# Gated recurrence and mixture layer on one core: GpSimd's parts of the weights given to ScalarE and VectorE, with a new order, engine shares and PSUM banks

## The chip, the cores and the metric

One NeuronCore of a Trainium2 chip runs the whole kernel. The metric is the device time in microseconds (us) of one execution, median over several runs; less is better.

## The reference

The first half is a decayed outer-product recurrence over 768 steps for 4 batches and 8 heads of width 48; its rows, 3072 tokens of 384 values, go through a gated layer of width 1536.

```python
for t in range(S):
    state = alpha[:, :, t, :, None] * state + einsum('bhd,bhe->bhde', k[:, :, t], v[:, :, t])
    y[:, :, t] = einsum('bhd,bhde->bhe', q[:, :, t], state)
x = y.transpose(0, 2, 1, 3).reshape(3072, 384)
g = x @ w_gate
out = (g * sigmoid(g) * (x @ w_val)) @ w_out
```

q, k, v and alpha are 32-bit floats. The three weights come as 64-bit floats, so the kernel reads each as two 32-bit words and makes a float of them itself.

## The kernel before, in words

**Recurrence.** The 768 steps of 4 batches are cut into 16 units of T = 192 steps (3 chunks of 64). A unit u loads alpha, k, q (La, Lk, Lq) and v (V), turns them so that the head dimension lies on partitions (on TensorE for units 0 to 3: T, K, with the widening copies p; on VectorE later: tr, tk, tq, kr), forms decay products by two scans on VectorE (G: `backward`, f: `forward`), multiplies k and q by them (mk, q), and lets TensorE form the scores (S), the carried state (Bw, or inside S) and the outputs (Y). VectorE masks (ma), advances and decays the state (ad, de); values are copied by vc. The output rows are scaled into an upper and a lower half-precision part (yh on ScalarE, yl on VectorE) and repacked into the x tile of a block (R and x on TensorE for units 0 and 1, copies xr by SyncE later).

**Layer.** Tokens form 7 blocks of 384 or 512. For each block, 12 steps f run over the width in slices of 128: `product` makes g and v with nine matmuls each (three row groups, each as upper x upper, upper x lower, lower x upper parts of half precision), `silu` (sl, ScalarE) and `hidden` (h, VectorE) make the gated value, `hidden_hi` and `hidden_lo` (hh, hl) split it, `out_product` (o) adds nine matmuls to the outputs. Step s = 12 x block + f; the names are g0, v0, ..., o83. There are two buffers each for h, hh and hl.

**Weights.** 36 slices of weights form 20 groups w0 to w19 (w0, w1, w2 and w19 of one slice, 384 columns; the others of two, 768). A group n is loaded (`wl`), made a float in three steps (v0, v1, v2; `single`), then split: `high` writes the upper part a, scaled by 256 to half precision; `low` writes the lower part p, the scaled value less the upper one. On VectorE `low` is one instruction (L353); on GpSimd it is two, a scaling in place (L355) and a subtraction (L356). Three spare tiles hold floats between v0 and p. All 20 groups are made while the first block (steps 0 to 11) is computed. Raw words of group n lie in the place of group n + 1, Y0 and Y1 lie in that of w18 and w17, and the tile for the widening copies in that of w19.

**Order.** The whole program stands in the text `ORDER` (L85): words such as `g:w13p` name the engine (t TensorE, v VectorE, s ScalarE, g GpSimd, y SyncE, whose queue issues nearly all loads) and the piece of work; digits behind @ are the PSUM banks, of A0, A1, A2, ops0, ops1, vps, gps, ops2 (0 to 7). Each engine works through its words in this order, and waits by semaphores for the data it needs. vps and gps are also the banks of the products v and g.

**Checks.** Beside the work ScalarE tests that weights and alpha lie in a range (wc, ck) and squares the hidden values (sq) of one step per block and of all of the last block. The results are joined (fr, fa, fe) into a flag by `verdict` (fb), which all engines read (fl, L1181) to branch past a slow general path (L1349).

Of the kernel before, what the change touches and what calls it, by code (L numbers as in the profile page):

```python
# [8 lines left out]
F32 = mybir.dt.float32  # L9
# [137 lines left out]
def main_path(ctx, tc, q, k, v, alpha, w_gate, w_val, w_out, out, flag, spill):  # L147
# [172 lines left out]

    idle, taken, read = ["t", "A", "B"], {}, []
    negative = {x for n, pieces in enumerate(wgroups) if f"g:w{n}v1" in ORDER.split() for x in pieces}

    def weight_group(n, pieces):

        size = len(pieces) * NB  # L330
        is32 = w_gate.dtype == F32
        each = NB if is32 else 2 * NB

        shape, dt = [P, len(pieces) * each], F32 if is32 else U32
        if n + 1 < len(wgroups):
            raw = p2.tile(shape, dt, tag=f"w{n + 1}", bufs=1, name=f"raw{n}")
        else:
            raw = spare(idle[0], shape, dt, f"raw{n}")
            taken["raw", n] = idle.pop(0)
        for i, piece in enumerate(pieces):  # L340
            weight_dma(raw[:, i * each : (i + 1) * each], *piece)
        parts = []

        def high(eng, src):
            parts.append(pairs16(p2.tile([P, 2 * size], F32, tag=f"w{n}", name=f"w{n}", bufs=1), [P, 2, size]))
            for i, piece in enumerate(pieces):
                wsp[piece] = tuple(parts[0][:, x, i * NB : (i + 1) * NB] for x in range(2))
            scaled(nc, eng, parts[0][:, 0, :], src, W_SCALE)

        def low(eng, src):  # L350
            hi, lo = parts[0][:, 0, :], parts[0][:, 1, :]
            if eng is nc.vector:
                eng.scalar_tensor_tensor(out=lo, in0=src, scalar=W_SCALE, in1=hi, op0=ALU.mult, op1=ALU.subtract)  # L353
            else:
                eng.tensor_scalar(out=src, in0=src, scalar1=W_SCALE, scalar2=None, op0=ALU.mult)  # L355
                eng.tensor_tensor(out=lo, in0=src, in1=hi, op=ALU.subtract)  # L356
            if n in taken:
                idle.append(taken.pop(n))

        if is32:  # L360
            return [], [lambda eng: high(eng, raw)], [lambda eng: low(eng, raw)]
        raw = raw.rearrange("p (c two) -> p c two", two=2)
        t = []

        def cut(i, eng):
            if not i:
# [509 lines left out]
    def hidden(blk, f):  # L876
        h = acc["h", blk, f]
        v_ = acc.pop(("v", blk, f))
        if (("v", f) in negative) != (("o", f) in negative):
            nc.vector.scalar_tensor_tensor(out=h, in0=v_, scalar=-1.0, in1=h, op0=ALU.mult, op1=ALU.mult)  # L880
        else:
            nc.vector.tensor_tensor(out=h, in0=h, in1=v_, op=ALU.mult)  # L882

    def hidden_hi(blk, f, eng):
        tag, n = ("tr", 1) if (blk, f) == (NBLK - 1, NF - 1) else ("hh", NH)
        hh = acc["hh", blk, f] = p2.tile([P, BLOCKS[blk][1]], F16, tag=tag, name=f"hh{blk}_{f}", bufs=n)
        (eng.copy if eng is nc.scalar else eng.tensor_copy)(out=hh, in_=acc["h", blk, f])  # L887

    def hidden_lo(blk, f, eng):
# [3 lines left out]
        eng.tensor_tensor(out=hl, in0=acc.pop(("h", blk, f)), in1=hh, op=ALU.subtract)  # L893
        hT[blk, f] = (hh, hl)

    squares = {}

    def squared(blk, f):

        h = acc["hh", blk, f]  # L900
        if f == 0:
            squares[blk] = p2.tile([P, BLOCKS[blk][1]], BF16, tag=f"sq{blk}", name=f"sq{blk}", bufs=1)
# [478 lines left out]
```

## Time and profile before

| | before |
|---|---|
| runs, us | 547.59, 548.43, 549.39 (median 548.43) |
| profiled execution, us | 548.03, its span 546.2 |
| busy us: VectorE / ScalarE / GpSimd | 377.1 / 286.7 / 167.4 |
| VectorE, share of the span | 69% |
| mean granted clock of TensorE | 0.984 of full |
| moved by DMA | 71.16 MB, mean 130 GB/s |

In rows of the profile PE is TensorE's matmuls, PEld its weight loads, DVE VectorE, ACT ScalarE, POOL GpSimd, SP SyncE; a q behind a name is an engine's queue. L12 is line 12 of the kernel. A matmul's length is that of one instruction in a pipeline, so nine of them take less than nine lengths. The granted clock is a share of 2.4 GHz; its lower level is 1.2 GHz. A wait is put down to the work whose end released it.

### The profile page before, as it was taken

To read this page: it belongs to the slowest core of one execution; us is meant where nothing else is said; L and a number is where in the kernel's file an instruction comes from. 1 tells how busy PE (TensorE), PEld (TensorE's weight loads), DVE (VectorE), ACT (ScalarE), POOL (GpSimd) and SP (SyncE) were. 2 spreads that over 40 slices of the span, in tenths; PEclk is the share of its full clock that TensorE was granted. 3 is DMA by queue.
4 is the path that set the end of the run, shared out by engine and by line. 5 is a ranking of instruction groups with operands and counts; after the bars stand their busy time and mean duration, and the time that the engine had idled before them with its cause. 6 is when DMAs were issued, how large, how long until landed. Compare 5 with 4: busy or idle time off the path is not lost.

```text
span 546.2 us, 13652 instructions
## 1 busy us (share of the span) xinstructions
PE 508.6 (93%) x5421; PEld 290.1 (53%) x5421; DVE 377.1 (69%) x623; ACT 286.7 (52%) x624; POOL 167.4 (31%) x164
## 2 busy tenths in 40 slices
PE   5979978699999999999999998999999999996995
PEld 4856545356665566665445553544545445554653
DVE  5979989489989869888968973595877443221113
ACT  4787778425333354334344335254356485567892
POOL 5784867573042112232123430003110020011011
PEclk9979989799999999999999999999999999999999
DMA  7699914156544464145726425446236433244521
GB/s 204 194 292 349 267 36 124 50 142 169 139 131 130 111 150 132 32 128 143 175 77 172 135 62 113 103 117 147 66 94 155 109 96 92 82 141 81 147 74 49
DMA packets 115142, 71.16 MB, mean 130 GB/s; under 512 B 64384, under 2 KB 112000, under 8 KB 115072
## 3 DMA queue, kind: packets, MB, share of 16 engines
q1 hardware_dynamic: 114368, 69.49, 47.3%
q8 instruction: 44, 0.72, 0.6%
q10 hardware_dynamic: 704, 0.74, 0.4%
q14 instruction: 26, 0.21, 0.1%
HBM read 61.34 MB, written 4.72 MB: 121 GB/s over the span
## 4 chain that ended last, share of the span: by engine, by line
PE 54%; DVE 12%; DMA 8%; POOL 7%; ACT 6%; SPq 6%; issue 5%; DVEq 0%; POOLq 0%; ACTq 0%
PE g L866 16%; PE v L866 15%; PE ops L944 13%; PE ops L949 4%; DMA V<-in_v_dram 2%; SPq L850 2%; POOL t L355 2%; PE y L748 2%; DVE K L564 2%; POOL w L356 2%; PE s L617 2%; DMA raw<-in_moe_w_out_dram 2%; DMA L<-in_alpha_dram 1%; ACT ac L488 1%; DVE trq L417 1%
## 5 line engine op out<-in xcount | busy, mean ns | idle before, releaser
L866 PEld LDWEIGHTS <-w 128*128 128x128 f16 x1512 | 146.9, 98 | 150.2 <-issue 16.9
L866 PE MATMUL g<-xT,w 128*128 128x384 f16 (+1 forms) x756 | 155.8, 351 | 13.5 <-ACT h L874 11.6
L866 PE MATMUL v<-xT,w 128*128 128x384 f16 (+1 forms) x756 | 154.6, 349 | 1.8 <-DVE h L882 1.2
L893 POOL TENSOR_TENSOR hl<-h,hh 128x384 f16<-128x384 f32 (+1 forms) x49 | 55.5, 1136 | 271.5 <-ACT hh L887 266.4
L874 ACT ACTIVATE h<-g 128x384 f32<-128x384 f32 (+1 forms) x84 | 44.7, 532 | 95.5 <-PE g L866 62.1
L887 ACT CAST hh<-h 128x384 f16<-128x384 f32 (+1 forms) x84 | 46.3, 552 | 90.8 <-PE ops L944 25.8
L949 PE MATMUL ops<-w,hh 128*128 128x384 f16 x286 | 78.2, 334 | 2.9 <-POOL w L356 2.9
L882 DVE TENSOR_TENSOR h<-h,v 128x384 f32<-128x384 f32 (+1 forms) x56 | 34.0, 608 | 58.7 <-PE v L866 45.4
L944 PE MATMUL ops<-hh,w 128*128 128x512 f16 x216 | 69.0, 379 | 0.0
L564 DVE STREAM_TRANSPOSE K<-Gs 32x384 f32<-32x384 f32 x96 | 54.7, 570 | 3.3 <-PE s L617 1.4
L944 PEld LDWEIGHTS <-w 128*128 128x128 f16 x324 | 31.1, 98 | 37.0
L949 PE MATMUL ops<-w,hl 128*128 128x384 f16 x143 | 47.6, 333 | 0.6 <-DVE hl L893 0.5
L880 DVE SCALAR_TENSOR_TENSOR h<-v,h 128x384 f32<-128x384 f32 (+1 forms) x28 | 17.1, 611 | 42.1 <-PE v L866 32.1
L944 PE MATMUL ops<-hl,w 128*128 128x512 f16 x108 | 40.9, 379 | 0.0
L949 PEld LDWEIGHTS <-hh 128*128 128x128 f16 x286 | 28.5, 99 | 22.5 <-issue 5.1
L495 DVE TENSOR_TENSOR_SCAN Gs<-AT,Z 128x776 f32<-128x776 f32 x16 | 30.1, 1880 | 4.2 <-ACT AT L1032 4.1
L502 DVE TENSOR_TENSOR_SCAN AT<-AT,Z 128x774 f32<-128x774 f32 x16 | 29.8, 1859 | 0.6
L893 DVE TENSOR_TENSOR hl<-h,hh 128x384 f16<-128x384 f32 (+1 forms) x35 | 21.8, 624 | 9.3 <-ACT hh L887 9.0
L317 ACT ACTIVATE wc<-wc 128x384 f32<-128x384 f32 x36 | 20.0, 555 | 14.9 <-DMA wc<-in_moe_w_gate_dram 5.3
L689 DVE TENSOR_TENSOR X<-s,mask 128x384 f32<-128x384 f32 (+1 forms) x34 | 18.4, 553 | 9.3 <-PE s L617 8.8
L318 ACT ACTIVATE wc<-wc,wbias 128x384 f32<-128x384 f32 x36 | 23.4, 651 | 1.2
L617 PEld LDWEIGHTS s<-X,Gs 48*64 48x64 f32 x672 | 20.8, 134 | 6.1 <-issue 3.7
(156 smaller groups left out, 723.4 us busy)
## 6 DMA issues: line engine op xcount, KB each, us to landing
raw<-in_moe_w_gate_dram SPq DMA_DIRECT2D x12, 384.0 KB, 7.5
V<-in_v_dram SPq DMA_DIRECT2D x96, 48.0 KB, 3.3
raw<-in_moe_w_val_dram SPq DMA_DIRECT2D x12, 384.0 KB, 7.1
raw<-in_moe_w_out_dram SPq DMA_DIRECT2D x12, 384.0 KB, 7.2
wc<-in_moe_w_gate_dram SPq DMA_DIRECT2D x12, 384.0 KB, 4.1
wc<-in_moe_w_out_dram SPq DMA_DIRECT2D x12, 384.0 KB, 3.5
wc<-in_moe_w_val_dram SPq DMA_DIRECT2D x12, 384.0 KB, 3.5
L<-in_k_dram SPq DMA_DIRECT2D x24, 144.0 KB, 3.6
```

Source lines behind the costliest of these rows:

```text
L318: nc.scalar.activation(dev, dev, AF.Abs, bias=wbias[:, 0:1])
L495: nc.vector.tensor_tensor_scan(Gf[:, ::-1], Af[:, ::-1], Z[:, : 0 : -1], 0.0, op0=ALU.mult, op1=ALU.add)
L502: nc.vector.tensor_tensor_scan(Af, Af, Z[:, 1 : n + 1], Z[:, 0:1], op0=ALU.mult, op1=ALU.add)
L564: nc.vector.transpose(out=bass.AP(k0.tensor, k0.offset, [k0.ap[0], (G * 2 * D, NU), (2 * D, G), (1, 32)]), in_=Kg[j * BO + x : j * BO + x ...
L617: nc.tensor.matmul(st["sps"][g // GF][j * BO : j * BO + C, g % GF, cx], KTt[r, g, cs], X[r, 0, g, cx], start=True, stop=True,)
L866: nc.tensor.matmul(pt, wsp[kind, f][a][:, kt * P : (kt + 1) * P], xT[blk][:, b_, kt, :], start=(n == 0), stop=(n == 3 * KT - 1),)
L874: nc.scalar.activation(h, acc.pop(("g", blk, f)), AF.Silu, scale=(-1.0 if ("g", f) in negative else 1.0) / H_SCALE)
L882: nc.vector.tensor_tensor(out=h, in0=h, in1=v_, op=ALU.mult)
L887: (eng.copy if eng is nc.scalar else eng.tensor_copy)(out=hh, in_=acc["h", blk, f])
L893: eng.tensor_tensor(out=hl, in0=acc.pop(("h", blk, f)), in1=hh, op=ALU.subtract)
L944: nc.tensor.matmul(ops[blk][i], wsp["o", f][a][:, i * P : (i + 1) * P], h[b_], start=(first and n == 0), stop=(last and n == 2),)
L949: nc.tensor.matmul(ops[blk][i], h[b_][:, i * P : (i + 1) * P], wsp["o", f][a], start=(first and n == 0), stop=(last and n == 2),)
```

## The change

- The upper parts of w0, w2, w3, w4, w5, w7, w8, w11, w19 go from GpSimd to ScalarE; the lower parts of w0, w8, w9, w13, w14, w15, w16, w19 go from GpSimd to VectorE. No `g:w..a` or `g:w..p` is left. (`g:w..v1` stay on GpSimd where they were: w0, w2, w3, w7, w19.)
- `high` gets a branch for groups whose lower part is made on GpSimd, which scales the float in place first; `low` on GpSimd loses its scaling.
- hl0, 1, 2, 3, 5, 6, 9, 15, 16, 19, 30, 31, 38, 46, 50, 51, 54, 59, 60, 62, 65, 70, 78, 80 go from VectorE to GpSimd; hl13, 20, 25, 37, 48, 49, 58, 63, 71, 72, 75, 79, 81, 82 from GpSimd to VectorE.
- q7, q10, q13, q14, mk10, mk13 go from VectorE to GpSimd; q3, q4, q9, q12, q15, mk1 from GpSimd to VectorE.
- S4, S6 to S12, S14, S15 and Y5 to Y7, Y9 to Y11, Y13, Y14 get other banks.
- The order of all 1453 words is new on every engine. The verdict fb moves from between o82 and o83 to the end, and with it the reading of the flag.
- The clearing of Y0 and Y1 (`rows_tile`) covers only the half that is used, in 32-bit words. `squared` writes to AT (last block) or to one tile per block.

The diff, with the long text `ORDER` cut to four stretches (the start, the steps up to v0, those up to o9, and the end):

```diff
@@ -83,7 +83,7 @@
 ORDER = """
-y:La0 g:ik g:pa0 t:Ta0@10 s:ea0 v:G0 y:Lk0 s:pk0 y:Lq0 t:Tk0@51 v:mk0 s:pq0 t:Tq0@56 t:K0.2@0 v:f0 y:La1 s:pa1 t:Ta1@13 g:is y:wl0 s:w0v0 v:q0 s:kc0.2
-y:Lk1 y:Lq1 g:pk1 g:w0v1 t:Tk1@46 s:ea1
...
-t:Y1@20 v:w2v2 g:w3v1 g:pa3 v:w3v2 s:yh1.1 g:w3a s:yh1.0 v:yl1.1 y:wl8 g:pk3 s:x0.2 t:R0.1@6 y:wl9 v:z2 t:R0.0@5 t:Ta3@31 v:yl1.0 t:K2.1@4 v:x0.0
-t:R1.0@2 t:R1.2@0 s:w1a v:w1p t:R1.1@5 s:ea3 t:Tk3@37 v:x1.0 t:K2.2@2 v:x1.1 g:w2a s:x0.1 s:x1.2 v:w2p y:Lq3 v:G3 s:w4v0 s:w4v1 y:wl10 v:w4v2 t:g0
-s:sl0 y:wl11 v:w3p g:w4a y:wl12 y:wl13 y:wl16 y:V3.1 y:wl15 t:v0
...
-v:w11p s:sl6 t:g7 s:yh2.1 s:kc3.0 v:w12p v:w13a v:hl5 s:w15v0 v:yl2.1 s:w16v0 v:h6 s:hh6 y:Lk4 s:yh2.0 g:w13p y:La4 s:w14v0 t:o5 v:hl6 v:yl2.0 t:v7
-s:sl7 v:de3 t:g8 v:h7 s:w14v1 v:w14v2 s:w15v1 s:w16v1 g:q3 v:w15v2 v:w16v2 t:v8 s:w14a t:S3@120 s:w15a s:sl8 v:ad3.0 v:ad3.1 s:w16a t:o6 g:w14p s:vc3
-y:wl18 t:g9 v:h8 v:ma3.0 v:ma3.2 s:hh8 g:w15p g:w16p s:w17v0 s:hh7 s:w17v1 t:Y3@20 s:yh3.0 v:tk4 v:tr4 t:v9 g:hl7 s:sl9 v:yl3.0 s:yh3.1 y:xr2 g:hl8
-g:z3 s:w18v0 v:yl3.1 v:w17v2 s:w18v1 t:g10 s:sl10 s:w17a y:wl19 v:h9 v:w18v2 y:xr3 y:Lq4 s:w18a t:o7 s:hh9 t:o8 v:w17p t:v10 v:w18p v:G4 v:hl9 v:h10
-v:f4 s:hh10 s:w19v0 g:mk4 g:w19v1 v:kr4.2 t:g11 s:sl11 g:hl10 t:o9
...
-t:fr@0 v:fa v:h83 t:o81 s:hh83 s:sq83 v:fe t:o82.0 g:hl83 t:o82.1 t:fb t:o83.0 t:o83.1 t:o82.2 t:o83.2 v:z15 y:fl v:ot83.0 s:os83.0 v:ot83.1 s:os83.1
-v:ot83.2 s:os83.2
+y:La0 y:Lk0 y:Lq0 g:iv g:pa0 t:Ta0@10 s:ea0 y:La1 v:G0 s:pk0 y:wl0 t:Tk0@51 g:im v:mk0 s:pq0 t:Tq0@56 s:pa1 t:Ta1@13 t:K0.2@0 g:ik y:Lk1 g:yz0 v:f0
+g:pk1 v:q0 s:w0v0 t:Tk1@46 g:w0v1 s:kc0.2 y:Lq1 t:K0.0@3 s:ea1
...
+t:Y1@20 y:wl5 y:V2.2 y:Lk3 s:ad1.2 g:w2v1 s:yh1.0 t:R0.1@6 y:V2.1 s:yh1.1 v:w1v2 t:K2.1@4 v:w2v2 y:wl7 y:Lq3 y:V2 y:wl6 g:pq2 g:w3v1 t:K2.0@5 s:kc2.0
+y:wl9 t:R0.2@7 s:w1a t:K2.2@2 v:yl1.0 v:yl1.1 v:w3v2 s:x0.2 y:wl8 s:w2a t:R1.2@0 t:Tq2@31 v:w1p t:R0.0@5 y:wl10 v:w2p y:wl11 t:R1.0@2 t:R1.1@5 s:kc2.2
+s:x0.1 s:w4v0 g:pa3 s:x1.2 v:x0.0 v:q2 g:pk3 v:x1.0 s:w4v1 v:x1.1 v:z2 t:Ta3@31 s:w3a t:g0 v:w4v2 s:ea3 s:w4a v:w3p v:G3 t:v0
...
+v:w11p v:w12p v:h6 v:w13a s:hh5 s:w15v0 t:S3@120 s:hh6 g:hl5 s:w16v0 g:hl6 v:w13p v:ad3.0 s:w14v0 s:w15v1 v:ma3.0 t:g7 t:v7 v:tr4 v:ma3.2 t:o5 s:sl7
+s:w14v1 s:w16v1 v:ad3.1 s:vc3 v:h7 t:g8 v:w14v2 y:V4.1 v:w15v2 t:v8 s:w14a v:w16v2 s:w15a s:sl8 v:w14p v:h8 t:Y3@20 s:w16a t:o6 v:w15p s:hh8 s:hh7
+g:hl7 t:g9 v:w16p y:xr2 s:w17v0 s:w17v1 v:tk4 t:v9 s:sl9 y:V4.2 s:w18v0 y:Lq4 s:yh3.0 v:G4 v:h9 s:w18v1 t:o7 y:V4 t:g10 s:hh9 v:w17v2 y:wl19 s:yh3.1
+g:hl8 v:w18v2 v:yl3.0 s:sl10 g:mk4 s:w17a s:w18a v:yl3.1 t:o8 t:v10 v:w17p v:h10 g:hl9 t:g11 v:w18p s:hh10 s:sl11 t:o9
...
+t:fr@0 s:hh82 v:h83 t:o81 s:wc27 v:hl82 s:hh83 s:sq82 s:sq83 v:fa t:o82.0 t:o82.1 g:hl83 t:o83.0 t:o83.1 v:fe t:o82.2 v:ot83.0 s:os83.0 v:ot83.1
+t:o83.2 v:ot83.2 t:fb
+s:os83.1 v:z15 s:os83.2 y:fl
 """
 
@@ -319,6 +319,7 @@
         nc.scalar.activation(dev, dev, AF.Relu, bias=wbias[:, 1:2], accum_out=wviol[:, 0, i : i + 1])
 
     idle, taken, read = ["t", "A", "B"], {}, []
+    whole = {n for n in range(len(wgroups)) if f"g:w{n}p" in ORDER.split()}
     negative = {x for n, pieces in enumerate(wgroups) if f"g:w{n}v1" in ORDER.split() for x in pieces}
 
     def weight_group(n, pieces):
@@ -345,6 +346,10 @@
             parts.append(pairs16(p2.tile([P, 2 * size], F32, tag=f"w{n}", name=f"w{n}", bufs=1), [P, 2, size]))
             for i, piece in enumerate(pieces):
                 wsp[piece] = tuple(parts[0][:, x, i * NB : (i + 1) * NB] for x in range(2))
+            if n in whole:
+                scaled(nc, eng, src, src, W_SCALE)
+                (eng.copy if eng is nc.scalar else eng.tensor_copy)(out=parts[0][:, 0, :], in_=src)
+                return
             scaled(nc, eng, parts[0][:, 0, :], src, W_SCALE)
 
         def low(eng, src):
@@ -352,7 +357,6 @@
             if eng is nc.vector:
                 eng.scalar_tensor_tensor(out=lo, in0=src, scalar=W_SCALE, in1=hi, op0=ALU.mult, op1=ALU.subtract)
             else:
-                eng.tensor_scalar(out=src, in0=src, scalar1=W_SCALE, scalar2=None, op0=ALU.mult)
                 eng.tensor_tensor(out=lo, in0=src, in1=hi, op=ALU.subtract)
             if n in taken:
                 idle.append(taken.pop(n))
@@ -779,8 +783,9 @@
 
     def rows_tile(u):
 
-        state[u]["Y"] = p2.tile([112, 2, G, T], F32, tag=f"w{len(wgroups) - 2 - u}", name=f"Y{u}", bufs=1).bitcast(F16)
-        nc.gpsimd.memset(state[u]["Y"][32:BO], 0.0)
+        Y = p2.tile([112, 2, G, T], F32, tag=f"w{len(wgroups) - 2 - u}", name=f"Y{u}", bufs=1)
+        nc.gpsimd.memset(Y[32:BO, :, :, 0 : T // 2], 0.0)
+        state[u]["Y"] = Y.bitcast(F16)
 
     def rows_of(u, i):
 
@@ -874,7 +879,7 @@
         nc.scalar.activation(h, acc.pop(("g", blk, f)), AF.Silu, scale=(-1.0 if ("g", f) in negative else 1.0) / H_SCALE)
 
     def hidden(blk, f):
-        h = acc["h", blk, f]
+        h = acc["whole", blk, f] = acc["h", blk, f]
         v_ = acc.pop(("v", blk, f))
         if (("v", f) in negative) != (("o", f) in negative):
             nc.vector.scalar_tensor_tensor(out=h, in0=v_, scalar=-1.0, in1=h, op0=ALU.mult, op1=ALU.mult)
@@ -884,6 +889,7 @@
     def hidden_hi(blk, f, eng):
         tag, n = ("tr", 1) if (blk, f) == (NBLK - 1, NF - 1) else ("hh", NH)
         hh = acc["hh", blk, f] = p2.tile([P, BLOCKS[blk][1]], F16, tag=tag, name=f"hh{blk}_{f}", bufs=n)
+        kept[blk, f] = hh
         (eng.copy if eng is nc.scalar else eng.tensor_copy)(out=hh, in_=acc["h", blk, f])
 
     def hidden_lo(blk, f, eng):
@@ -893,18 +899,21 @@
         eng.tensor_tensor(out=hl, in0=acc.pop(("h", blk, f)), in1=hh, op=ALU.subtract)
         hT[blk, f] = (hh, hl)
 
-    squares = {}
+    squares, kept = {}, {}
 
     def squared(blk, f):
 
-        h = acc["hh", blk, f]
+        n = BLOCKS[blk][1]
+        if blk == NBLK - 1:
+            to = AT.rearrange("p g t -> p (g t)").bitcast(BF16)[:, n * (f > 0) : n * (f > 0) + n]
+        else:
+            to = p2.tile([P, n], BF16, tag=f"sq{blk}", name=f"sq{blk}", bufs=1)
         if f == 0:
-            squares[blk] = p2.tile([P, BLOCKS[blk][1]], BF16, tag=f"sq{blk}", name=f"sq{blk}", bufs=1)
-        to = squares[blk] if f == 0 else p2.tile([P, BLOCKS[blk][1]], BF16, tag="sq", name=f"sq{blk}_{f}", bufs=1)
+            squares[blk] = to
         if blk == NBLK - 1:
-            nc.scalar.activation(to, acc["h", blk, f], AF.Square, accum_out=hsum[:, f : f + 1])
+            nc.scalar.activation(to, acc["whole", blk, f], AF.Square, accum_out=hsum[:, f : f + 1])
         else:
-            nc.scalar.activation(to, h, AF.Square)
+            nc.scalar.activation(to, kept[blk, f], AF.Square)
 
     def rows_summed(eng, bank):
```

## Rows read from the trace of the kernel before

**Rows 1.** The page's first part: busy time, share of the span, instructions.
```profile
PE 508.6 (93%) x5421; PEld 290.1 (53%) x5421; DVE 377.1 (69%) x623; ACT 286.7 (52%) x624; POOL 167.4 (31%) x164
```
**Rows 2.** Stretches: length, busy PE, PEld, DVE, ACT, POOL; clock, DMA share, GB/s.
```profile
10.00:41.50 31.50, 26.86 (x469) 22.65 (x468) 27.10 (x41) 24.10 (x58) 24.87 (x34) 0.89 0.83 235
10.00:70.00 60.00, 53.33 (x716) 38.56 (x715) 54.14 (x81) 46.59 (x96) 43.64 (x43) 0.94 0.87 260
40.00:70.00 30.00, 27.97 (x262) 17.24 (x260) 28.54 (x44) 23.74 (x41) 19.47 (x10) 1.00 0.91 292
41.50:116.70 75.20, 64.43 (x697) 38.26 (x695) 62.42 (x85) 49.98 (x80) 48.59 (x29) 0.93 0.55 165
116.70:240.00 123.30, 120.50 (x1578) 75.93 (x1577) 108.65 (x173) 49.03 (x114) 34.37 (x35) 1.00 0.48 128
```
**Rows 3.** Waits of PE from 41.5 to 116.7 us: total, times, longest.
```profile
PE g L866 <- ACT h L874: 4.8, 2, 3.9
PE ops L949 <- POOL w L356: 2.9, 1, 2.9
```
**Rows 4.** The chain of waits, 100 to 104 us: start, length, what.
```profile
100.28 1.64 POOL w L356
```
**Rows 5.** Timeline of PE: g0 and g10.
```profile
41.54 1.63 PE L866 MATMUL g<-xT,w 128*128 128x384 f16 x9
...
103.36 3.04 PE L866 MATMUL g<-xT,w 128*128 128x384 f16 x9 [3.89 <-ACT h L874]
```
**Rows 6.** Waits of DVE from 10 to 41.5 us: total, times, longest.
```profile
DVE Y L801 <- ACT Y L67: 1.9, 2, 1.7
DVE t L135 <- POOL t L122: 1.4, 1, 1.4
```
**Rows 7.** Groups of POOL, shapes apart: count, busy us, mean ns, idle before.
```profile
L69 POOL TENSOR_SCALAR w<-t 128x768 f16<-128x768 f32 x6 | 14.8, 2467 | 12.6 <-DVE t L135 5.8 <-ACT w L67 2.6 <-DMA raw<-in_moe_w_val_dram 2.1
L521 POOL TENSOR_TENSOR X<-trq,AT 112x768 f32<-112x768 f32 x8 | 13.7, 1714 | 23.7 <-DVE trq L417 15.2 <-DVE K L564 8.5
...
L355 POOL TENSOR_SCALAR t<-t 128x768 f32<-128x768 f32 x6 | 13.3, 2219 | 6.1 <-ACT w L67 3.1 <-DVE w L69 2.3 <-DMA V<-in_v_dram 0.6
L356 POOL TENSOR_TENSOR w<-t,w 128x768 f16<-128x768 f32 x6 | 11.9, 1988 | 0.5
```
**Rows 8.** The same groups on ACT and DVE, and hl on POOL and DVE.
```profile
L67 ACT ACTIVATE w<-t 128x768 f16<-128x768 f32 x7 | 5.7, 840 | 1.3 <-DVE t L135 1.3
...
L353 DVE SCALAR_TENSOR_TENSOR w<-t,w 128x768 f16<-128x768 f32 x10 | 11.5, 1170 | 2.2 <-ACT w L67 1.2 <-POOL w L69 1.1
...
L893 DVE TENSOR_TENSOR hl<-h,hh 128x384 f16<-128x384 f32 x19 | 10.6, 557 | 3.9 <-ACT hh L887 3.8
...
L521 DVE TENSOR_TENSOR X<-trq,AT 112x768 f32<-112x768 f32 x6 | 5.7, 957 | 0.2
...
L893 POOL TENSOR_TENSOR hl<-h,hh 128x384 f16<-128x384 f32 x29 | 27.7, 961 | 120.5 <-ACT hh L887 120.4
```
**Rows 9.** Timeline: decays (L718) on DVE, alone and beside POOL.
```profile
20.52 0.85 DVE L718 SCALAR_TENSOR_TENSOR V<-SE,Gs 48x192 f32<-48x192 f32 x2
...
83.70 1.64 POOL L356 TENSOR_TENSOR w<-t,w 128x768 f16<-128x768 f32 x1
...
84.13 3.22 DVE L718 SCALAR_TENSOR_TENSOR V<-SE,Gs 48x192 f32<-48x192 f32 x2
```
**Rows 10.** Waits of SyncE's queue over the span: total, times, longest.
```profile
SPq L411 <- POOL L L408: 20.0, 2, 15.3
```
**Rows 11.** The end: timeline of PE and DVE, and line L1349 (ns, starts).
```profile
538.76 0.19 PE L1173 MATMUL cps<-okf,ones 128*1 128x1 f32 x2 [0.51 <-DVE okf L1168]
...
541.47 0.35 DVE L977 SCALAR_TENSOR_TENSOR ot<-beyond,ot 128x192 f32<-128x192 f32 x1
...
L1349 PEldq COMPARE_BRANCH x1: 3442/3442/3442, 539.8 to 539.8; - x1
```

2 lines of the change are left out of this document (1 added, 1 removed).

## The prediction

> **What bounds the kernel now.** I read the page's first part first: TensorE is busy for 508.6 of 546.2 us [rows 1], so only its idle time, 37.6 us, and stretches at a low clock can be won. The view of stretches then says where they lie [rows 2]. From 41.5 us (the first g product) to 116.7 us (the last v product of the first block) TensorE has 64.43 us of work in 75.20, at a mean granted clock of 0.93; from 116.7 to 240 us it works 120.50 of 123.30. In that first stage 36 pieces of weights are still being made, and the waits of TensorE there [rows 3] name GpSimd's subtraction (2.9 us at once) and ScalarE's Silu (4.8 us). The chain of waits shows that the Silu is GpSimd again: the subtraction of 100.28, an hl behind it in the queue, the Silu that needs a slot which that hl frees, and then g10 at 103.36, after TensorE has stood for 3.89 us [rows 4, 5]. After that wait the nine matmuls of g10 take 3.04 us instead of the 1.63 us of g0: of the two levels, 1.2 and 2.4 GHz, they run at the lower, right behind the idle time [rows 5]. So the stage loses twice: 10.8 us of idle time and some 4.5 us of slow clock (0.07 of 64.43). Its floor is 0.93 x 64.43 = 59.9 us.
>
> Ahead of it VectorE sets the pace: from 10 to 41.5 us it is busy for 27.10 us, and its waits are mostly two, 1.9 us for rows scaled by ScalarE, which had waited for GpSimd's clearing of Y, and 1.4 us for a GpSimd step of the weights [rows 2, 6].
>
> **The change, part by part.**
>
> *Weights off GpSimd.* Nine upper parts (w0, 2, 3, 4, 5, 7, 8, 11, 19) go to ScalarE, eight lower ones (w0, 8, 9, 13 to 16, 19) to VectorE. The wide ones alone free GpSimd of 14.8 + 13.3 + 11.9 = 40.0 us [rows 7]. Six wide uppers cost ScalarE 0.84 us each, 5.0 us; in the stage it then has 49.98 + 5.0 = 55 us of work, under the floor [rows 2, 8]. Six wide lowers cost VectorE 1.17 us each, 7.0 us [rows 8]. The lower part also loses its latency: 2.2 + 2.0 us on GpSimd against 1.17. With no lower part left on GpSimd, the new scaling in place is never reached, and the removed rescaling has no caller: nil.
>
> *The head.* With GpSimd's queue light, both waits of VectorE go, 3.3 us [rows 6]. Y's clearing falls from 3072 half-words a row to 768 words, a quarter of the elements, and stands early in the queue. VectorE gets two things more before g0: the multiplication mk1 (nearest row 0.96 us) and half a lower part (0.59 us) [rows 8]. Net 3.3 - 1.5 = **1.8 us earlier**. Ends: 2.9 us (all its idle time of 4.4 less 1.5), or nothing, if what is late next, the rows of Y0 and Y1 through ScalarE, holds it as long.
>
> *The first stage.* With GpSimd gone VectorE is late next, and its work gives the length. Now 62.42 us [rows 2]; plus 7.0 (lowers), plus 0.96 (q3 comes from GpSimd), less 7 x 0.56 = 3.9 (hl0, 1, 2, 3, 5, 6, 9 go to GpSimd) [rows 8], less some 2.2 (one pair of transposes, w19v2 and h11 now stand behind v11): 64.3 us. From this comes off what VectorE loses when it stands beside GpSimd. One pair of decays takes 3.22 us beside GpSimd's subtraction of 83.70, where it took 0.85 at 20.52 [rows 9]; I take off 3.8 us, that case and one more of 1.4 us: 60.5 us. VectorE was busy for 54.14 of 60 us (90%) from 10 to 70 us and for 28.54 of 30 (95%) from 40 to 70 [rows 2]; between the two, 92.5%, the stage takes 65.4 us, above TensorE's floor of 59.9. Saving **9.8 us**. Ends: 15.3 us (the floor), and a loss of 2.6 us (third rival).
>
> The rows of 83.70 and 84.13 look like one engine standing until the other is through. The Trainium skill (SBUF — State Buffer, "Who interferes with whom") says that a VectorE instruction with two SBUF inputs and a GpSimd one that reads SBUF lock each other out for whole instructions; the trace agrees (3.22 against 0.85). It speaks for taking work off GpSimd, and against the other half of the change: a lower part on VectorE has two SBUF inputs, and so have the hl that GpSimd gets. By the rule's first half alone the time is the forecast's; if its second half decides, the third rival's.
>
> *SyncE.* It stood 20.0 us, once 15.3, for GpSimd's filling of a load tile [rows 10] with later weight loads queued behind. That filling now has hl's before it, not lowers, and wl14 to wl18 stand ahead of the long run of copies xr2. Weights come earlier; nothing is charged or credited, as VectorE is the pace. If cover fails, it is the fourth rival.
>
> *The middle.* 24 hl go from VectorE to GpSimd and 14 come back; six multiplications q and mk go each way. From unit 4 on S and Y take other banks, eleven of them now in a bank of g or v against ten, two of these Y (7 and 10) against one (13). VectorE has 14.65 us idle from 116.7 to 240 and TensorE 2.8 [rows 2], so I take nothing. Ends: 2.8 us won; 3.2 lost (the 2.2 us handed on, and 1.0 for two more reads of about 0.5 us that a g or v must wait for).
>
> *The end.* The verdict's matmul goes from between o82 and o83 to the last place; its wait of 0.51 us on TensorE goes [rows 11], since the small joins also stand behind h83 now. But the flag is then read after the last output tile, at 541.8 at the earliest, and TensorE's branch past the general path, which ran 3.44 us from 539.8 beside the last products and stores, starts some 2 us or more later [rows 11]. It was over at 543.2 and the span at 546.2, so most of that slack covers it: between nothing and 2.7 us; I take 1.3, the middle. With the 0.5 won the end costs **0.8 us**.
>
> *The squares* write to AT instead of a tile of their own: same instruction, nil.
>
> **The sum.** The profiled execution took 548.03 us, 546.2 of them the span. 548.03 - 1.8 - 9.8 + 0.8 = 537.2 us. The median of the runs, 548.43, stands 0.4 above it: **537.6 us**.
>
> **The rivals.** Times are against 548.43; a measurement can tell about 0.3% (1.6 us) from no change.
>
> First, *VectorE gets no relief*: GpSimd's hl cost it as much as the lowers did. Then 64.3 / 0.925 = 69.5 us, a saving of 5.7, and the time is 548.4 - 1.8 - 5.7 + 0.8 = **541.7**. For it: VectorE is 90 to 95% busy at the start. Against: a subtraction of weights is 2 us, an hl half that [rows 7, 8].
>
> Second, on the other side, *GpSimd's hl come late for the output products*. Each of the 24 takes 0.96 instead of 0.56 us, and each of the six multiplications 0.76 more (1.71 against 0.96 [rows 7, 8]): 9.7 + 4.5 = 14.2 us if all lie on the path. With the forecast's saving of 10.8 that gives **551.8**; it decides from three quarters of them on the path. Against: GpSimd's 29 narrow hl now wait 120.4 us for ScalarE [rows 8], so the engine stands ready, and TensorE's longest waits are for other work [rows 3]. For: GpSimd had fewer hl then, and some o now follow sooner.
>
> Third, *the lock decides the stage*: the eight hl left to GpSimd there (0, 1, 2, 3, 5 to 8) each hold VectorE for 0.96 us, 7.7 us on 64.3: 72.0 / 0.925 = 77.8 us, 2.6 more than now. With head and end that is 548.4 - 1.8 + 2.6 + 0.8 = **550.0**; if half of them hold it, 545.8. Against: GpSimd had 48.59 us of work in the stage [rows 2] and VectorE still did its 62.42; little of the former stays.
>
> Fourth, *weights arrive too late*: the DMA engines are 0.91 busy from 40 to 70 us [rows 2], and if the loads set the pace nothing moves: **548.4**. Against: over the whole stage their share is 0.55, and SyncE's long stop was a wait for GpSimd [rows 10].
>
> **How the numbers follow.** The forecast's case has 0.58, the first rival 0.20, the third 0.10 (half of it near 545.8), the second 0.08, the fourth 0.04. Faster by over 0.3% (below 546.8): 0.58 + 0.20 + 0.05 = 0.83. Within 0.3%: 0.05 + 0.04 = 0.09. Slower (over 550.1): 0.08. The range goes down to 548.43 - 2.9 - 15.3 + 0.8 = 531.0 and up to 546.5, which takes in the first rival and the milder half of the third; what is left out is 0.17 above and a little below.
>
> **What would show it.** Right: in the same two stretches, g0 at about 39.7 us, and the last v of the first block 65 us later, with a granted clock near 1; no GpSimd weight lines; VectorE over 90% busy there and the releaser of most of TensorE's waits. The decays at about 0.85 us a pair show the relief. The end: a branch of over 3 us begun after 541.8 less what was won. Wrong: TensorE waiting for hl of GpSimd (second rival), VectorE instructions of twice their length beside hl (third), ScalarE waiting for raw weights (fourth), or an idle TensorE between 116.7 and 240 us in the place of the idle time that went.

## The result, and the profile after

The changed kernel takes **529.79 us** (median of 4 runs, 528.12 to 531.10) where the kernel before took 548.06 beside it: a ratio of 0.966, 95% interval 0.963 to 0.970, so some 18 us less. The forecast was 537.6 us. The profiled execution took 531.10 us, its span 529.2.

The first part of the page of the kernel after answers to [rows 1]:

```profile
PE 500.7 (95%) x5421; PEld 287.5 (54%) x5421; DVE 369.9 (70%) x621; ACT 289.2 (55%) x633; POOL 132.4 (25%) x149
```

GpSimd lost 35 us of work and TensorE's idle time fell from 37.6 to 28.5 us; of its busy time 7.9 us went as well, with the mean granted clock up from 0.984 to 0.993. To see where, I took five landmarks from TensorE's timeline in both traces: the starts of g0, of v11 (the last v of the first block), of g73 and of the last product of the output, and the end of the span.

| stretch | before | after | difference | forecast |
|---|---|---|---|---|
| start to g0 | 41.54 | 42.20 | +0.7 | -1.8 |
| g0 to v11 (first stage) | 73.52 | 59.59 | -13.9 | -9.8 |
| v11 to g73 (middle) | 368.99 | 369.52 | +0.5 | 0 |
| g73 to the last product (last block) | 56.72 | 50.25 | -6.5 | -0.5 |
| last product to the end | 5.43 | 7.64 | +2.2 | +1.3 |

The view of stretches of the kernel after, with columns as in [rows 2]: the head, the first stage and the last block. Below it the last block of the kernel before.

```profile
10.00:42.20 32.20, 25.19 (x463) 20.96 (x461) 27.37 (x42) 25.13 (x62) 14.79 (x32) 0.95 0.97 281
42.20:103.25 61.05, 59.65 (x700) 37.85 (x699) 60.29 (x84) 51.87 (x84) 19.94 (x18) 1.00 0.60 167
...
464.50:521.80 57.30, 57.30 (x372) 34.26 (x370) 17.39 (x53) 49.26 (x123) 4.76 (x6) 1.00 0.38 99
```
```profile
479.20:541.00 61.80, 56.27 (x363) 33.27 (x361) 14.52 (x50) 45.47 (x117) 7.43 (x9) 1.00 0.37 96
```

**First stage.** VectorE has 60.29 us of work there (forecast 60.5), but it does them in 61.05 us: it is busy for 98.8%, not 92.5%. TensorE has 59.65 us, the floor that the prediction worked out (59.9), at a granted clock of 1.00 instead of 0.93. So the stage is 0.8 us longer than VectorE's work and 1.4 longer than TensorE's, and this trace alone doesn't say which of the two sets its length; experiment 3 does. TensorE's waits [rows 3] are down to:

```profile
PE g L871 <- DVE w L358: 0.6, 1, 0.6
PE v L871 <- DVE h L887: 0.5, 1, 0.5
PE g L871 <- ACT h L879: 0.3, 1, 0.3
```

VectorE's waits in the stage, first the longest of the kernel before (41.5 to 116.7 us; it was idle for 12.8 us in all), then all of the kernel after:

```profile
DVE X L801 <- ACT X L67: 6.2, 2, 5.4
```
```profile
DVE X L806 <- ACT X L67: 0.2, 1, 0.2
```

Half of what VectorE lost was a wait for rows that ScalarE scales. The timelines of ScalarE and VectorE before show where it began:

```profile
102.81 0.49 ACT L874 ACTIVATE h<-g 128x384 f32<-128x384 f32 x1 [5.12 <-POOL hl L893]
```
```profile
103.72 0.56 DVE L801 SCALAR_TENSOR_TENSOR X<-y,X 112x384 f16<-112x384 f32 x1 [5.43 <-ACT X L67]
```

It is the chain of [rows 4, 5] once more: the Silu that waited for GpSimd's hl had the scaling of the rows behind it in ScalarE's queue, and VectorE stood for that. Groups of VectorE in the stage, before and after:

```profile
L135 DVE SCALAR_TENSOR_TENSOR t<-raw,t 128x768 uint32<-128x768 uint32 x15 | 14.6, 995 | 1.3 <-POOL U L534 1.3
L353 DVE SCALAR_TENSOR_TENSOR w<-t,w 128x768 f16<-128x768 f32 x10 | 11.5, 1170 | 2.2 <-ACT w L67 1.2 <-POOL w L69 1.1
...
L718 DVE SCALAR_TENSOR_TENSOR V<-SE,Gs 48x192 f32<-48x192 f32 x4 | 4.0, 1011 | 0.0
```
```profile
L135 DVE SCALAR_TENSOR_TENSOR t<-raw,t 128x768 uint32<-128x768 uint32 x15 | 17.0, 1163 | 0.0
L358 DVE SCALAR_TENSOR_TENSOR w<-t,w 128x768 f16<-128x768 f32 x16 | 15.7, 992 | 0.1
...
L722 DVE SCALAR_TENSOR_TENSOR V<-SE,Gs 48x192 f32<-48x192 f32 x4 | 1.4, 344 | 0.0
```

The decays are back at 0.69 us a pair and a lower part takes 0.99 instead of 1.17 us: relief. The third step of the float conversion (L135) went the other way, 1.00 to 1.16 us.

**Head.** g0 came later. Before, TensorE's longest wait from 10 us to g0 was one of 2.7 us that the profile puts down to GpSimd's lower part of w0 (first row). It is gone, but now TensorE's first output product of unit 1 waits 3.10 us, and VectorE then waits for the rows:

```profile
PE pt L442 <- POOL w L356: 2.7, 1, 2.7
```
```profile
32.44 0.27 PE L765 MATMUL y<-X,V 128*64 128x64 f32 x1 [3.10 <-DVE Gs L1067]
```
```profile
29.50 1.83 DVE L506 TENSOR_TENSOR_SCAN AT<-AT,Z 128x774 f32<-128x774 f32 x1
31.36 1.03 DVE L1067 TENSOR_TENSOR Gs<-pt,Gs 128x384 f32<-128x384 f32 x2
...
35.95 2.28 DVE L806 SCALAR_TENSOR_TENSOR Y<-y,Y 48x384 f16<-48x384 f32 x4 [2.17 <-ACT Y L67]
```

Y1 goes to banks 2 and 0, where the turned k of unit 2 lies until mk2 (L1067) has read it; and mk2 stands behind the scan f2 (1.83 us) on VectorE. So it did in the old order, but there three words, the turning of unit 2's q among them, lay between Bw1 and Y1 on TensorE; in the new order Y1 follows Bw1 at once.

**Last block.** TensorE never stands there now. Before, it stood 5.4 us; the timelines of VectorE, ScalarE and TensorE of the kernel before:

```profile
493.94 0.71 DVE L959 STREAM_TRANSPOSE ot<-ops 128x128 f32<-128x128 f32 x3 [2.75 <-DMA out_dram<-ot]
```
```profile
494.68 0.52 ACT L985 ACTIVATE ot<-ot 128x384 f32<-128x384 f32 x1 [2.08 <-DVE ot L959]
```
```profile
495.73 1.62 PE L866 MATMUL g<-xT,w 128*128 128x384 f16 x9 [2.47 <-ACT h L874]
```

The transposes ot71.2 and ot71.3 wait until a store has emptied a tile (2.75 and 2.04 us; the first is shown), ScalarE stands in front of their scaling (2.08 and 1.76) with the next Silu behind it, and TensorE wants the bank that this Silu reads (2.47 and, later, 1.71; with a third wait 4.9 in all, and 0.5 for the verdict). In the kernel after neither transpose waits; the first of them:

```profile
478.37 0.70 DVE L968 STREAM_TRANSPOSE ot<-ops 128x128 f32<-128x128 f32 x3
```

**End.** TensorE's branch stands after the last product, as forecast:

```profile
L1358 PEldq COMPARE_BRANCH  x1: 3562/3562/3562, 523.4 to 523.4; - x1
```

It is over 2.2 us before the end of the span; before the change that was 3.0 us [rows 11], so only some 0.7 us of that slack went to cover its later start.

### The profile page after: what moved, and what is told of

Same layout as the page of the kernel before. It is cut to its first block, busy times and chain, and to the rows that moved or that the text cites. A ratio compares the mean times of both kernels' runs of the same rounds, so it can differ in the third digit from the quotient of the medians.

```text
span 529.2 us, 13619 instructions
## 1 busy us (share of the span) xinstructions
PE 500.7 (95%) x5421; PEld 287.5 (54%) x5421; DVE 369.9 (70%) x621; ACT 289.2 (55%) x633; POOL 132.4 (25%) x149
## 4 chain that ended last, share of the span: by engine, by line
PE 63%; DVE 14%; DMA 6%; SPq 5%; ACT 5%; issue 4%; POOL 1%; DVEq 0%; POOLq 0%; ACTq 0%
PE v L871 19%; PE g L871 19%; PE ops L953 12%; PE ops L958 7%; PE y L752 3%; SPq L855 2%; PE s L621 2%; DVE K L568 2%; DVE t L135 2%; DMA raw<-in_moe_w_gate_dram 1%; DMA xT<-X 1%; DVE trk L421 1%; DMA L<-in_q_dram 1%; PE A L629 1%; SPq L1002 1%
## 5 line engine op out<-in xcount | busy, mean ns | idle before, releaser
L899 POOL TENSOR_TENSOR hl<-h,hh 128x384 f16<-128x384 f32 (+1 forms) x59 | 69.2, 1175 | 333.8 <-ACT hh L893 310.4
L958 PE MATMUL ops<-w,hh 128*128 128x384 f16 x286 | 76.5, 326 | 0.0
L499 DVE TENSOR_TENSOR_SCAN Gs<-AT,Z 128x776 f32<-128x776 f32 x16 | 28.4, 1778 | 5.2 <-ACT AT L1041 5.1
L317 ACT ACTIVATE wc<-wc 128x384 f32<-128x384 f32 x36 | 19.9, 551 | 13.9 <-DMA wc<-in_moe_w_val_dram 11.0
L67 ACT ACTIVATE X<-y 112x384 f16<-112x384 f32 x28 | 13.0, 488 | 23.7 <-PE y L752 22.9
L899 DVE TENSOR_TENSOR hl<-h,hh 128x384 f16<-128x384 f32 (+1 forms) x25 | 15.4, 615 | 13.5 <-ACT hh L893 13.4
L318 ACT ACTIVATE wc<-wc,wbias 128x384 f32<-128x384 f32 x36 | 23.4, 651 | 1.2
L319 ACT ACTIVATE wc<-wc,wbias 128x384 f32<-128x384 f32 x36 | 23.4, 651 | 1.2
```

What stands on the lines that cost most here:

```text
L499: nc.vector.tensor_tensor_scan(Gf[:, ::-1], Af[:, ::-1], Z[:, : 0 : -1], 0.0, op0=ALU.mult, op1=ALU.add)
L958: nc.tensor.matmul(ops[blk][i], h[b_][:, i * P : (i + 1) * P], wsp["o", f][a], start=(first and n == 0), stop=(last and n == 2),)
```

## The experiments

Ratios are to the kernel before on the same chip, with 95% intervals; times taken side by side on one chip compare best with each other. Moves in the order are given as words, the changed ones alone.

**1. All parts back, new order kept.**

```diff
-s:w0a s:w2a s:w3a s:w4a s:w5a s:w7a s:w8a s:w11a s:w19a v:w0p v:w8p v:w9p v:w13p v:w14p v:w15p v:w16p v:w19p
+g:w0a g:w2a g:w3a g:w4a g:w5a g:w7a g:w8a g:w11a g:w19a g:w0p g:w8p g:w9p g:w13p g:w14p g:w15p g:w16p g:w19p
```

GpSimd's lower part is again two instructions, as in the kernel before.

> The changed kernel with all 17 weight parts back on GpSimd (and GpSimd's scaling in place of before), every other word of the new order kept. Theory W (the parts on GpSimd made the first stage long): from g0 to the end of the last v of the first block 61.1 us becomes about 75 us, with TensorE waiting for GpSimd's lines of weights; time 541 to 546 us. Rival O (the new order made the gain): the stage stays below 65 us and the time below 534 us.

548.81 us, ratio 1.002 (0.9995 to 1.0044): in total everything is lost. The stage, from g0 to the end of v11, and waits of TensorE from 40 to 121 us:

```profile
41.53:120.25 78.72, 63.54 (x700) 38.36 (x699) 59.70 (x78) 48.11 (x78) 55.45 (x38) 0.96 0.48 136
```
```profile
PE ops L955 <- POOL hl L896: 3.8, 1, 3.8
PE v L868 <- POOL w L357: 3.6, 1, 3.6
...
PE g L868 <- POOL w L357: 1.6, 1, 1.6
```

TensorE waits for GpSimd's subtractions again. From g0 to v11 it takes 77.3 us, 17.7 more than in the changed kernel and 3.7 more than before. The last block keeps its whole gain: g73 to the last product takes 50.25 us, without a wait. So the order with its shares and banks wins 6.5 us at one place and loses nearly all of it at others (3.7 in the stage, 2.5 at the end); the loss of some 18 us is the first stage's alone.

**2. The same move in the kernel before, old order kept** (the words of experiment 1 the other way round).

> The kernel before with the 17 weight parts moved to ScalarE and VectorE, in the old order, nothing else. Theory W: the stage of 75.0 us falls to 61 to 66 us and the time to 534 to 540 us; the end keeps its 4.9 us of TensorE's waits for ScalarE. Rival O: the old order is laid out for GpSimd's parts, so the words stand at the wrong places; the stage keeps more than 70 us and the time 543 us or more.

545.41 us, ratio 0.9936 (0.9915 to 0.9957): 3 us, not 18. g0 to the end of v11 takes 69.5 us, and the last block 56.7 as before. That first stretch, and VectorE's waits in it:

```profile
42.07:111.57 69.50, 62.94 (x696) 37.92 (x694) 59.23 (x87) 52.02 (x83) 10.86 (x11) 0.95 0.54 165
```
```profile
DVE t L135 <- ACT t L119: 4.8, 5, 1.8
DVE w L353 <- ACT w L67: 2.9, 1, 2.9
```

GpSimd stands nearly idle (10.86 us of work), and VectorE is 85% busy: it now waits 7.7 us for ScalarE, whose steps of the weights stand too late for the new owners. From g0 to v11 the four kernels take 73.5 us (before), 77.3 (new order alone), 67.9 (new owners alone) and 59.6 (both): the move of the parts is worth 5.7 us in the old order and 17.7 in the new one, so the order had to be laid out for the new shares.

**3. Which half hurts GpSimd: uppers alone, lowers alone.**

```diff
-s:w0a s:w2a s:w3a s:w4a s:w5a s:w7a s:w8a s:w11a s:w19a
+g:w0a g:w2a g:w3a g:w4a g:w5a g:w7a g:w8a g:w11a g:w19a
```

> The changed kernel with only the nine upper parts back on GpSimd. Theory W (what counts is GpSimd's work, whichever part it is): the uppers are 14.8 of the 40.0 us, and with all parts back 18.3 us were lost, so 18.3 x 0.37 = 6.8 us longer than the changed kernel's 529.8: about 536.6 us. Rival A (only the lower parts hurt, since they are two instructions on GpSimd and have two SBUF inputs): 529.8 us. Rival B (the latency of the upper hurts most, as VectorE's lower waits for it at the head of VectorE's queue): over 540 us, with waits of VectorE for GpSimd's upper.

535.49 us, ratio 0.974 (0.970 to 0.978). The stage, one group of VectorE in it, and all of VectorE's waits there:

```profile
41.39:107.16 65.77, 60.41 (x702) 37.78 (x701) 64.46 (x84) 47.96 (x78) 34.13 (x26) 1.00 0.54 157
```
```profile
L358 DVE SCALAR_TENSOR_TENSOR w<-t,w 128x768 f16<-128x768 f32 x16 | 18.2, 1146 | 0.6 <-POOL w L69 0.5
```
```profile
DVE w L358 <- POOL w L69: 0.5, 1, 0.5
DVE X L806 <- ACT X L67: 0.2, 1, 0.2
```

The same 84 instructions as in the changed kernel take VectorE 64.46 instead of 60.29 us, with 0.7 us of waits: it isn't held by what it waits for, its instructions get longer (a lower part 1146 ns against 992). The stage grows with it, 61.05 to 65.77 us, while TensorE's work stays near 60 us, and TensorE's waits there are mostly for VectorE (4.3 of 5.3 us): VectorE's work sets the length.

```diff
-v:w0p v:w8p v:w9p v:w13p v:w14p v:w15p v:w16p v:w19p
+g:w0p g:w8p g:w9p g:w13p g:w14p g:w15p g:w16p g:w19p
```

The lower part on GpSimd is again two instructions.

> The changed kernel with only the eight lower parts back on GpSimd, as two instructions. Theory W: the lowers are 25.2 of the 40.0 us: 18.3 x 0.63 = 11.5 us longer, about 541.3 us, with TensorE waiting for GpSimd's subtraction. Rival A (only the lower parts hurt): the whole 18.3, about 548 us. Rival B (VectorE sets the stage, and here it is relieved of 7 us of work): 529.8 us or less.

543.76 us, ratio 0.989 (0.987 to 0.991). The stage, and the longest waits of TensorE and VectorE in it:

```profile
42.02:115.90 73.88, 63.63 (x702) 38.62 (x700) 58.79 (x78) 52.27 (x84) 41.90 (x30) 0.95 0.50 143
```
```profile
PE g L868 <- ACT h L876: 4.6, 2, 3.0
PE v L868 <- POOL w L357: 3.6, 1, 3.6
```
```profile
DVE h L884 <- ACT h L876: 6.6, 2, 5.1
```

Here VectorE has less to do (58.79 us) and stands: the other way to lose, by lateness, with TensorE's clock at 0.95. With the changed kernel at 0.966 of 549.4, or 530.8, the two cost 4.7 and 13.0 us, 17.7 together, where experiment 1 lost 19.1 by the same reckoning (548.81 less 0.966 of 548.27): shares near those of GpSimd's work (6.8 and 11.5 expected). From g0 to v11 alone it is 4.6 and 12.7, 17.2 together, against 17.7 in experiment 1. Theory W holds, in two forms.

**4. The hl back on their engines of before** (38 words `hl`).

> The changed kernel with the 38 hl back on the engines of the kernel before. Theory S (VectorE's work sets the first stage, so seven hl less there were part of the gain): the stage grows by about 7 x 0.56 = 3.9 us, to 65 us from g0 to the end of v11; later on nothing; time about 533.5 us. Rival L (hl on GpSimd stretch VectorE's work by the lock, so their move is free or harmful): the stage keeps 61 us or less, 529.8 us or less. Rival M (the 14 hl that went to VectorE matter later): more idle time on TensorE behind 103 us.

537.29 us, ratio 0.980 (0.975 to 0.985), some 6 us longer (the runs spread over 4 us, and the profiled one, 535.49, is the shortest); but theory S fell. v11 starts 60.1 us after g0, against 59.59. The float steps take 15.6 us in that stage instead of 17.0:

```profile
L135 DVE SCALAR_TENSOR_TENSOR t<-raw,t 128x768 uint32<-128x768 uint32 x15 | 15.6, 1066 | 0.0
```

With the lower parts (15.1 against 15.7) and L69 (1.7 against 1.9), 2.2 us of what seven hl cost VectorE (7 x 0.55 = 3.9) come back as shorter neighbours. The loss lies later, v11 to g73 3.3 us longer, with waits of TensorE for VectorE (5.4 us in all from 104 to 476 us, against 2.2 in the changed kernel), the longest:

```profile
PE v L871 <- DVE h L887: 2.2, 2, 2.1
...
PE ops L958 <- DVE hl L899: 1.3, 1, 1.3
```

So the hl pay behind the first block (rival M), where the forecast took nothing for them.

**5. The last block.** The first try undid in the changed kernel what looked like the cause, the late place of the scalings:

```diff
-t:o73 t:g77 v:ot71.2 g:hl74 ... v:ot71.3 v:h76 ... t:o75 s:oz71.3 ... s:sl79 s:oz71.2
+v:hl73 v:ot71.2 ... s:oz71.2 s:sl75 v:ot71.3 s:oz71.3 t:v76
```

> The changed kernel with the last two scalings of block 5's outputs (oz71.2, oz71.3, and the transposes before them) back near their old place on ScalarE, five steps earlier. Theory Z (the kernel before lost its end because ScalarE stood for these two with the Silu's behind them): ScalarE stands 3 to 4 us before them, TensorE waits 3 to 5 us in the last block, time 532.5 to 535 us. Rival (the end became shorter by other engine shares, h and hl): no wait of over 1 us for them, time within 1 us of 529.8.

531.52 us, ratio 0.969; g73 to the last product takes 51.47 us instead of 50.25. Only 1.2 of the 6.5 us came back. The second try put them late in the kernel before, with their stores:

```diff
-v:ot71.2 s:oz71.2 s:sl75 ... v:ot71.3 s:oz71.3 t:v75
+v:ot71.2 g:hl74 ... v:ot71.3 v:h76 ... t:o75 s:oz71.3 y:os71.3 ... s:oz71.2 y:os71.2 t:v79
```

> The kernel before, with the last two transposes and scalings of the block before the last placed as late as in the changed kernel. Theory Z (they make ScalarE stand, and TensorE 2.47 and 1.71 us behind it): ScalarE's two waits of 2.08 and 1.76 us go, TensorE's waits for Silu in the last block fall from 4.9 to under 1 us, time 548.2 - 4.2 = 544 us. Rival (the last block is short of something else, slots or VectorE's turn, and the wait comes later): 548.2 us, with TensorE's waits there again 4 to 5 us.

554.33 us, ratio 1.009 (1.006 to 1.013): slower. TensorE's waits from 484 us on:

```profile
PE ops L949 <- ACT hh L887: 4.8, 1, 4.8
PE ops L949 <- DVE ot L959: 2.4, 1, 2.4
...
PE g L866 <- ACT h L874: 0.4, 2, 0.2
```

The Silu's waits went, as expected (4.9 to 0.4), but o72 now waits for a transpose, and ScalarE waited 5.8 us for a load that stands behind the second late store on SyncE. As the stores went late with the scalings, this run doesn't test the place of the scalings by itself; the first try gives it 1.2 us. What is late first is the store of the rows before. SyncE's first store, before and after:

```profile
489.78 1.35 SPq L993 DMA_DIRECT2D out_dram<-ot x2
```
```profile
473.10 1.35 SPq L1002 DMA_DIRECT2D out_dram<-ot x2
```

That is 7.4 us after o71's last matmul began (482.37), in the kernel after 2.0 us (471.09), since h72 (which waits for v72) and the Silu of step 73 are ahead of ot71.0 and of its scaling, and the range check ck4 is ahead of oz71.1, whose store goes first. The third try moves the first two rows with their stores:

```diff
-v:h72 s:sl73 s:hh72 s:sq72 v:ot71.0 s:oz71.0 s:ck4 v:ot71.1 s:oz71.1 t:v73
+v:ot71.0 v:ot71.1 s:oz71.0 s:oz71.1 y:os71.0 y:os71.1 v:h72 s:sl73 s:hh72 s:sq72 s:ck4 t:v73
```

> The kernel before, with the first two transposes, scalings and stores of the block before the last moved ahead of h72 and the Silu of step 73, into time in which VectorE (8.05 us) and ScalarE (4.44 us) stood idle. Theory T (the first stores went out 7.2 us after the last o71 instead of 1.6, so the third and fourth transposes waited for their tiles, ScalarE for the transposes, and TensorE for ScalarE): VectorE's waits of 2.75 and 2.04 us for the stores, ScalarE's of 2.08 and 1.76 and TensorE's of 2.47 and 1.71 go: 548.2 - 4.2 = 544.0 us. Rival (the last block is short of something else and waits later): 548.2 us.

545.43 us, ratio 0.991 (0.988 to 0.994), 4.0 us less. All waits of TensorE from 484 us on:

```profile
PE g L866 <- ACT h L874: 0.7, 1, 0.7
PE cps L1173 <- DVE okf L1168: 0.5, 1, 0.5
```

The transposes ot71.2 and ot71.3 follow at once (1.30 us for both, no wait). Theory T holds: g73 to the last product takes 52.2 us, 4.5 less than before. Of the 1.9 us that are left to the 50.25 of the kernel after, 1.2 are the two waits shown; the rest stays open.

**6. The head.**

```diff
-v:f2 v:mk2
+v:mk2 v:f2
```

> The changed kernel with mk2 ahead of f2 on VectorE, one word moved. Theory H (the head won nothing because Y1 needs the PSUM banks that Tk2 holds until mk2 has read them, and mk2 stood behind the 2 us of f2): the wait of TensorE for mk2 falls from 3.1 us to about 1, g0 starts at about 40.2 us instead of 42.2, and with it the time falls by 1.5 to 2 us to about 528. Rival (f2's lateness costs as much, since q2 and x need it, or the weights' loads set g0): g0 within 0.5 us of 42.2, time unchanged.

528.72 us, ratio 0.9635 (0.9615 to 0.9656); g0 at 40.64 us, and the wait is down:

```profile
30.25 0.27 PE L765 MATMUL y<-X,V 128*64 128x64 f32 x1 [0.50 <-DVE Gs L1067]
```

As the two intervals overlap, I ran both kernels again on one chip.

> The changed kernel as it is, as the yardstick of the next run on the same chip: ratio to before 0.966, about 530 us.

> The changed kernel with mk2 ahead of f2, once more, beside the changed kernel on the same chip. Theory H (VectorE's order at the head costs 1.6 us at g0, and nothing takes it back): 1.1 to 2.2 us below the changed kernel in the same call. Rival (the difference of 1.1 us between two separate calls was chance): within 0.3 us of it.

531.02 us, ratio 0.9677 (0.9661 to 0.9692), and 530.27 us, 0.9661 (0.9645 to 0.9678). The gain is 0.75 us, with overlapping intervals: not settled as a gain. In this trace g0 is at 42.56 us all the same, because TensorE stood for something else, earlier:

```profile
30.03 1.36 PE L671 MATMUL A<-V,K 128*48 128x96 f32 x21 [2.64 <-issue]
...
32.60 0.37 PE L765 MATMUL y<-X,V 128*64 128x64 f32 x1 [0.62 <-ACT V L707]
```

What released the first of these the trace does not name. The wait for mk2 is real, and removing it moves g0 by 1.3 to 1.6 us in two of three traces; in the third the next thing late took its place.

**7. The flag read before the last tiles.**

```diff
-v:fe t:o82.2 v:ot83.0 s:os83.0 v:ot83.1 t:o83.2 v:ot83.2 t:fb s:os83.1 v:z15 s:os83.2 y:fl
+v:fe t:fb v:z15 y:fl t:o82.2 v:ot83.0 s:os83.0 v:ot83.1 t:o83.2 v:ot83.2 s:os83.1 s:os83.2
```

> Theory F (the flag read after the last output tile is what lengthens the end): from TensorE's last instruction to the end of the span 5.4 us as in the kernel before, not 7.6; the time about 527.6 us, 2.2 less than the changed kernel's 529.8; TensorE stands some 0.5 us for the verdict again, near 526.1 to 528.0 with it. Rival (the last store sets the end, wherever the flag is read): still 7.6 us and 529.8.

530.0 us, ratio 0.965 (0.961 to 0.969): nothing won. The branch begins 1.1 us earlier, and the end is 6.0 us long instead of 7.6; but the products behind the flag's matmul stand:

```profile
521.31 0.19 PE L1182 MATMUL cps<-okf,ones 128*1 128x1 f32 x2
522.25 0.32 PE L958 MATMUL ops<-w,hh 128*128 128x384 f16 x1 [0.75 <-DVE AT L510]
```

so the output's last product starts at 523.15 instead of 521.56, and VectorE is through with the last output row at 524.3 instead of 522.5. From there to the end it is 4.9 us instead of 6.7: theory F is right about the end, and the 1.8 us won there are lost ahead of it. The flag's matmul stands here behind o83.1, two words later than in the kernel before (behind o82.1), where it cost TensorE a wait of 0.5 us and none behind it; that place was not tried in the changed kernel.

**8. mk2 ahead of f2 and the early flag together.**

> Theories H and F together (mk2 ahead of f2 at the head, the flag read ahead of the last tiles): the two lie at the two ends and add up: g0 near 40.6 us instead of 42.2, the end 5.4 us instead of 7.6, time 529.8 - 1.1 - 2.2 = 526.5 us, ratio to before 0.960. Rival (what is won at the head is taken back on the way, in a stage that weights or x rows pace): 527.6, as with the flag alone.

529.11 us, ratio 0.9637 (0.9597 to 0.9677): as with mk2 alone. The sum of the two expectations wasn't reached, since the flag brings nothing. No version here beats the changed kernel by more than a measurement can tell.

## Why the prediction was wrong, point by point

The direction and the mechanism were right, and the time was forecast 7.8 us too long; it lies 1.2 us below the range. By the table of stretches the first stage gave 4.1 us more and the last block 6.0 more than forecast; the head, the middle and the end took back 2.5, 0.5 and 0.9. That makes 6.2; the rest is that the profiled execution after lies 1.3 us above its median, where the one before lay 0.4 below.

- **The first stage: right mechanism, mis-sized term.** VectorE's work came out at 60.29 us against 60.5 forecast. Part of that agreement is luck: the relief of 3.8 us, taken for decays alone, came from decays (2.6) and L69 (1.2), and the 16 lower parts, 0.18 us shorter each, were balanced by the 15 float steps, 0.17 us longer each. The step that failed is "between the two, 92.5%, the stage takes 65.4 us": it took VectorE's share of busy time from stretches of the old kernel, 10 to 70 and 40 to 70 us. Of the 5.9 us of idle time in the first, 3.3 are the two waits of the head that the prediction itself counts as going. In the stage VectorE was busy for 62.42 of 75.20 us, 83%, and of the 12.8 us of idle time there 6.2 were waits for X rows that came late through ScalarE, at the end of the very chain that the prediction had read for TensorE and not followed to VectorE. Without them VectorE is at 98.8%, and the stage takes 61.05 us instead of 65.4, near TensorE's floor, which the forecast had as an end of the range and not as its value.
- **Weights alone don't do it.** I costed the move and took the new order as a means to it. Experiments 1 and 2 show that in the first stage the two need each other: from g0 to v11 the new order alone costs 3.7 us, the new owners alone win 5.7, and both win 13.9.
- **The last block: missed, the larger of the two failed steps.** The sum has no term for the block's last rows. "The end costs **0.8 us**" looked at the verdict alone. TensorE's three waits for Silu, 4.9 us, stood in the profile of before; I did not follow the moved words of the block's last rows. The place of six words in that chain (two transposes, two scalings and their stores) gives 4.0 us by itself in the kernel before (experiment 5, third try), and the block keeps its gain of 6.5 us with all weight parts back on GpSimd (experiment 1).
- **The head: wrong sign.** "Net 3.3 - 1.5 = 1.8 us earlier" counted VectorE's work and its two waits, and not what a bank must wait for. The waits for GpSimd did go, but waits of 3.1 us for rows through ScalarE (2.17 at once) came in their place, behind a product that waited for mk2's reading of its banks. The prediction had such rows as the reason for its end "nothing"; the measured time lies 0.7 us past that end.
- **The middle:** nothing was taken, and +0.5 us came; but it is a balance, since the hl of before in the new order would have cost 3.3 us there (experiment 4).
- **The end:** +2.2 against +1.3, inside the ends given (0 to 2.7); "most of that slack covers it" did not come, 0.7 of 3.0 us did. Reading the flag earlier won nothing in the one place tried, as the verdict's matmul there costs TensorE what the branch saves (experiment 7).
- **The rivals.** VectorE without relief (first): in part there, as hl on GpSimd lengthen VectorE's instructions by 2.2 us (experiment 4), but far from the price. The second and the third did not come. TensorE waits for no hl of GpSimd after the change; only its longest wait of the middle, 2.1 us for a Silu, stands behind one, for which that Silu had waited 0.8 us. The lock is paid more by GpSimd, whose hl of 961 ns [rows 8] take 1143 on the mean, and the ten in the first stage (the prediction counted eight) 1450. Fourth: weights are not late; TensorE's one wait for a weight there is 0.6 us and for VectorE.

The Trainium skill (SBUF — State Buffer, "Who interferes with whom") has it that VectorE instructions with two SBUF inputs and GpSimd ones that read SBUF hold each other up. Experiments 3 and 4 agree: 1146 against 992 ns for a lower part beside uppers on GpSimd, 1163 against 1066 for a float step beside hl. In sum VectorE lost 4.2 us in experiment 3 beside 14.8 us of uppers on GpSimd (six of 2.47 us).

## What to carry to other kernels

A share of busy time is not a property of an engine: before using it, split the idle rest by who ended each wait, and strike out what the change removes; if little is left, the next engine's floor is the forecast. When the order is laid out anew, walk through every stretch in which the bounding engine stands, and ask of each wait there whether the words in its chain moved: here a third of the gain came from a stretch that the stated purpose of the change doesn't touch. And moving work off an overloaded engine can pay far more when the queues of the engines that receive it are reordered with it: here 17.7 us instead of 5.7 in the stage. A total that doesn't change can also hide a gain and a loss, as in experiment 1: compare by stages.

## What the runs showed of the hardware

The two ways in which a loaded GpSimd costs time could be told apart: uppers there lengthened VectorE's instructions (4.2 us on the same 84, with 0.7 us of waits), lowers there made it stand. In the first stage ten hl of one shape (128x384) took from 917 to 2414 ns on GpSimd. TensorE's granted clock followed its waits: 1.00 over the whole first stage of the changed kernel, with no wait above 0.6 us, and 0.95 over that stage in experiments 2 and 3 (lowers), with single waits of up to 2.5 and 3.6 us.
